# Moving the attention of the even chunks between the FFN groups of a fused mLSTM and squared-ReLU FFN kernel

## The chip, the cores and the metric

The kernel runs on one core of a Trainium2 chip. A core has five engines, each with its own in-order instruction queue: PE (TensorE, matrix multiplication), DVE (VectorE), ACT (ScalarE), POOL (GpSimd) and SP (SyncE, which here only issues transfers). POOL issues transfers too, from the same queue that holds its arithmetic. The metric is the device time of one execution in microseconds (us).

## The reference

```python
# per step t, for each of 4 x 8 (batch, head) pairs, D = 40, S = 768
m_new  = max(f + m, i)
C = exp(f + m - m_new) * C + exp(i - m_new) * v k^T
n = exp(f + m - m_new) * n + exp(i - m_new) * k
y = sigmoid(o) * (C q) / max(|n q|, 1)
# then x = y as (3072, 320), and
h = max(x @ w_in, 0)          # (3072, 2048)
out = (h * h) @ w_out         # (3072, 320)
```

All is float32; the two weights arrive as 64-bit floats and are rounded in the kernel.

## The kernel before, in words

Tokens are cut into 24 chunks of 128 (six for each batch). A chunk's recurrence is computed as masked attention inside the chunk plus a state C that is carried from one chunk to the next. Two chunks make a group of 256 tokens, of which there are 12; the FFN works by group. FFN1 (x times w_in) and FFN2 (h² times w_out) use a Strassen-like scheme, whose sums of inputs and weights other engines prepare.

The main loop (from line 1430 on) is an order of work written out by hand. It walks a list `parts` of quarter steps: four steps of FFN2 for one group, then four of FFN1 for the group two further on, and so on. Each four steps are a window, and each window also carries one chunk `s` of attention: **even chunks go with an FFN2 window, odd chunks with an FFN1 window** (`fast` in the code). `at` is the quarter step, 0 to 3. [...]

For one chunk the attention has these parts:

- `pair_up` (line 338; the DMAs L343) copies keys and queries into DRAM in another order. From chunk 10 on POOL issues it, four DMAs for a chunk. `load_squares` (L398, SP, four DMAs) reads them back as 32x32 squares, and `turn_kq` (L405, DVE) transposes them. There are two such buffers, for even and odd chunks.
- `load` (L363, L365, L375) brings keys and values: seven DMAs, issued by POOL.
- `load_A` (L429, two DMAs on SP) brings the decay logarithms A. `decays` (L496, four instructions on ACT) takes their exponentials, `mask` (L478, two on POOL) masks A, `weigh` (L509, eight on ACT) turns A into weights and calls `values` (L530, POOL), `decay_C` (L767, POOL) decays the state.
- `scores` (L586, 32 PE instructions) multiplies keys and queries, `weighted` (L608, two on DVE) multiplies scores and weights, `scale_q` (L762, DVE) scales the queries.
- `attend_begin` (L800, L820, L831) and `attend_end` (the same lines) are the two halves of the product with values and state. Between them stands L791, a tiny DVE instruction that reads the first half's result and so keeps the second half behind it. After `attend_end` DVE turns and copies the result (L854, L861).
- `store_num` (L869), `load_num` (L874), both SP, take the result through DRAM; `normalise_turned` (L886 to L899, DVE) divides; `store_rows` (L927) and `load_rows` (L932) take it through DRAM again; `turn_squares` (L939, DVE) transposes it to be the FFN's input. `sums_of_x` (L1125, L1128; five POOL instructions) then makes the sums `xs` of a group that FFN1 of the next window needs.

All attention matmuls have 64 rows or fewer, and so have the last 64 of the 320 input rows of FFN1 (`ffn1_rows`, L1166). The rest of the FFN (L1133 for FFN1, L1057 for FFN2) uses 128 x 128 matmuls. FFN1 does two halves of a group in one window: `ffn1_open` (four products X, Y, V, Z of eight instructions; Y and V read sums made by POOL, Y reads `xs[3]`), then `ffn1_close` (three products, and `ffn1_rows` for the second half). FFN2 does seven products of 16 instructions in four steps; in step 0 ACT copies the first product out of its bank (L1077) before step 1 adds to that bank.

Around the change the order per window, PE's part first, is:

- even window: `scores(s)` at the top, FFN2 step 0, `attend_begin(s)`, `scores(s+1)`, `attend_end(s)`, FFN2 steps 1 to 3.
- odd window: open, `attend_begin(s)`, `ffn1_rows`, `attend_end(s)`, close; open, close with `ffn1_rows`.
- POOL in an even window: `mask(s+1)`, `decay_C(s+1)`, `load(s+3)` at step 1; `values(s+1)` at step 2; `sums_of_x`, `pair_up(s+3)`, `pair_up(s+4)`, `load(s+4)` at step 3; then in the odd window `mask(s+1)` for the next even chunk, and so on.
- SP in an even window: `store_num`, `load_num`, `load_squares(s+2)`, `load_A(s+2)`; output; `store_rows`, `load_rows`; output. In an odd window: `store_num`, `load_num`, `load_squares(s+2)`; `store_rows`, `load_A(s+2)`, `load_rows`.

Of the kernel before, what the change touches and what calls it, by code (L numbers as in the profile page):

```python
# [29 lines left out]
def kernel(  # L30
# [30 lines left out]
    NB = S // P  # L61
    NT = B * NB
# [340 lines left out]
    def turn_kq(s):  # L403
        t = kqT_b[s % NKT][:].rearrange("p n j t -> p (n j t)")
        nc.vector.transpose(t, t)  # L405
# [192 lines left out]
    def weighted(s):  # L598
        d = st[s]
        d["P"] = []  # L600
        for i in range(2):
            heads = slice(i, H, 2)
            t = d["W"][:, heads, :] if s < ROT else d["W"][:, i::2, DP:]
            if s < W_IN:
                at = 2 * H * P + W * (2 * (s % 2) + i)
                t = flat_c[:, at : at + W].rearrange("p (j t) -> p j t", j=PR)
            d["P"].append(t)
            nc.vector.tensor_tensor(t, d["sc"][i], d["W"][:, heads, :] if s < ROT else t, op=ALU.mult)  # L608
# [522 lines left out]
    def blocks(to, lhsT, rhs, q, start):  # L1131
        for n in range(4):
            nc.tensor.matmul(  # L1133
                to[:, n, :], lhsT=lhsT[:, 4 * q + n, :], rhs=rhs, start=(start and n == 0), stop=True,
                skip_group_check=True,
            )
# [17 lines left out]
    def ffn1_rows(g, q, first):  # L1154
        xT, xs = st["xT", g], st["xs"]
        X, Y, V, Z = st["f1"]
        lo, hi = HALVES
        pairs = (
            ((X, lo, xT[lo, 0, 2, :], False), (Y, hi, xT[hi, 1, 2, :], first)),
            ((V, lo, xT[lo, 1, 2, :], first), (Z, hi, xs[hi, 1, :], False)),  # L1160
        )
        for pair in pairs:
            for n in range(4):
                for cols in HALVES:
                    for to, rows, rhs, start in pair:
                        nc.tensor.matmul(  # L1166
                            to[cols, n, :], lhsT=w_in2[rows, 4 * q + n, cols], rhs=rhs,
                            start=(start and n == 0), stop=True, skip_group_check=True,
                        )

    def ffn1_close(g, q, begun):
        xT, xs = st["xT", g], st["xs"]
        (X, Y, V, Z), (U2, U4) = st["f1"], st["U"]
        g4 = st["g2", g][:, 8 * q : 8 * q + 8, :].rearrange("p (n two) t -> p n two t", two=2)
        t0, t1 = slice(0, P), slice(P, 2 * P)
        blocks(X, F12, xT[:, 0, 1, :], q, False)
        blocks(Y, F21, xs[:, 2, :], q, not begun)
        blocks(V, WS[3], xT[:, 1, 1, :], q, not begun)
        if not begun:
            ffn1_rows(g, q, False)  # L1180
        tt = nc.vector.tensor_tensor
        nc.scalar.activation(g4[:, :, 0, t0], X[:], AF.Relu)  # L1182
        tt(U2[:], U2[:], Y[:], op=ALU.add)
        tt(g4[:, :, 1, t1], U4[:], Y[:], op=ALU.add)
        tt(g4[:, :, 0, t1], U4[:], V[:], op=ALU.add)
        tt(g4[:, :, 1, t0], U2[:], Z[:], op=ALU.subtract)
        st["open"] = g4
# [16 lines left out]
    def do(f, s):  # L1204
        if 0 <= s < NT:
            f(s)
# [97 lines left out]
    for u in range(8):  # L1304
        s = 2 + u // 2
# [114 lines left out]
    for g in range(NG):  # L1420
        parts += [(2, g, i) for i in range(4)]
        if g + 2 < NG:
            parts += [(1, g + 2, i) for i in range(4)]
    ROUNDED = (17, 18)
    assert ROUNDED[-1] == len(pieces)

    for n, (which, g, i) in enumerate(parts):
        s, at = NB + n // 4, n % 4
        if n == len(ROUNDED):
            brought.close()  # L1430
            late = ctx.enter_context(tc.tile_pool(name="late", bufs=1, side="right"))
        even = s % 2 == 0
        fast = which == 1
        if n == 2:
            half_tanh(6)
            half_tanh(7)
        if at == 0 and even:
            do(scores, s)
            if n > 0:
                do(turn_kq, s + 1)  # L1440
            do(weighted, s)
        if n == 0:
            turn_kq(7)
            pair_up(8)
            load_rows(4)
            rounding.words()
            rounding.join()
        if at == 1:
            do(attend_begin, s)
            if n == 5:  # L1450
                sums_of_weights(3)
            if even:
                do(lambda s: scores(s, ("h", "h")), s + 1)
            if fast:
                ffn1_rows(g, 0, True)
            do(attend_end, s)
            do(decays, s + 1)
            do(mask, s + 1)
            if not even and not fast:
                do(turn_kq, s + 1)  # L1460
            do(decay_C, s + 1)
            if not fast and not even:
                do(turn_squares, s - 1)
            if even and s > NB:
                do(load, s + 3)
            do(store_num, s)
            if n == 1:
                normalise_turned(5)
                store_rows(5)
                turn_squares(4)  # L1470
            if n == 5:
                load_rows(6)
            do(load_num, s)
            if n == 1:
                load_rows(5)
                weigh(7, masked=True)
                sums_of_win(2)
            do(load_squares, s + 2)
            if even:
                do(load_A, s + 2)  # L1480
        if n == 3:
            load_o(8)
            load_o(9)
            sums_of_weights(0)
        if n == 8:
            sums(1, slice(0, NPAIR), (3,))
        if n == 9:
            sums(1, slice(0, NPAIR), (4,))
            sums_of_weights(2)
            turn_squares(6)  # L1490
        if which == 2 and i == 3 and g == NG - 2:
            sums(g + 1, slice(0, NPAIR), (2,))
        if which == 2 and g > 1 and i < 2:
            sums(g, slice(0, NPAIR), (3 + i,))
        if at == 3 and even and NB < s and s // 2 - 1 < NG:
            sums_of_x(s // 2 - 1)
        if at == 2 and not fast:
            if even and n > 2:
                do(turn_squares, s - 1)
            do(scale_q, s + 1)  # L1500
        if at == 3:
            if s % 4 == 3:
                for r in range(s + 1, min(s + 5, NT) if n > 7 else 10):
                    half_tanh(r)
        if n == 10:
            half_tanh(10)
            half_tanh(11)
        if fast:
            if i % 2:
                if n == 7:  # L1510
                    sums(1, slice(0, NPAIR), (2,))
                ffn1_close(g, i // 2, i == 1)
                if at == 1:
                    do(turn_kq, s + 1)
                    if n > 5:
                        do(turn_squares, s - 1)
            else:
                ffn1_open(g, i // 2)
                if i == 0 and g > 2:
                    sums(g - 1, slice(0, NPAIR), (2,))  # L1520
            if at == 2:
                do(scale_q, s + 1)
            if n == 6:
                sums(1, slice(0, NPAIR), (1,))
        elif g == 0:
            ffn2(i)
        else:
            ffn2_fast(g, i)
        if at == 2:
            if n > 2:  # L1530
                do(lambda s: weigh(s, masked=True), s + 1)
            ffn1_square()
            if even:
                do(weighted, s + 1)
            do(normalise_turned, s)
            do(store_rows, s)
            if n == 2:
                pair_up(9)
                turn_squares(5)
                sums_of_x(2)  # L1540
                load(8)
            if not even:
                do(load_A, s + 2)
            if n > 2:
                do(load_o, s + 5)
                do(load_rows, s)
            if s == NB + 1:
                pair_up(s + 3)
        if n in (5, 6):
            load(4 + n)  # L1550
            load_o(5 + n)
        if even and at == 3 and s > NB:
            do(pair_up, s + 3)
            do(pair_up, s + 4)
        if even and at == 3 and s > NB:
            do(load, s + 4)
        if n == 4:
            sums_of_weights(1)
        if n == 3:
            turn_halves()  # L1560
        if n in (12, 25):
            spread_slots(2 + n // 25)
        if at == 0:
            ffn1_square()
        if n < len(ROUNDED):
            while rounding.done < ROUNDED[n]:
                rounding.step()
# [30 lines left out]
```

## Time and profile before

| what | value |
|---|---|
| time, median of 3 runs | 485.88 us (484.6 to 485.91) |
| profiled execution's own time | 488.72 us |
| its span (first to last instruction) | 487.0 us |
| TensorE clock granted | 1.00 |
| PE busy | 475.4 us, 98% of the span |
| DVE busy | 339.5 us, 70% |
| ACT busy | 243.3 us, 50% |
| POOL busy | 227.1 us, 47% |
| DMA moved | 69.93 MB, mean 144 GB/s |

A time in the profile is counted from the first instruction. "PE" rows are matmuls, "SPq" rows are transfers being issued by SP, and an issue on POOL stands among POOL's own rows. In the timeline a row merges neighbouring instructions of one line; its columns are start, length (both us), engine, line, operation, destination <- sources, shape and count. The chain is followed back from the last instruction, at each step to what released it.

The windows that the change touches begin at 125.3 us (FFN2 with chunk 8) and end at 421.2 us (FFN2 with no chunk left). A pair of windows, even and odd, takes 36.2 to 37.0 us in the profile, except one pair in which PE stood still for 1.88 us at 224.8 us with no releaser shown.

### The profile page before, as it was taken

To read this page: it belongs to the slowest core of one execution; us is meant where nothing else is said; L and a number is where in the kernel's file an instruction comes from. 1 tells how busy PE (TensorE), PEld (TensorE's weight loads), DVE (VectorE), ACT (ScalarE), POOL (GpSimd) and SP (SyncE) were. 2 spreads that over 40 slices of the span, in tenths; PEclk is the share of its full clock that TensorE was granted. 3 is DMA by queue.
4 is the path that set the end of the run, shared out by engine and by line. 5 is a ranking of instruction groups with operands and counts; after the bars stand their busy time and mean duration, and the time that the engine had idled before them with its cause. 6 is when DMAs were issued, how large, how long until landed. Compare 5 with 4: busy or idle time off the path is not lost.

```text
span 487.0 us, 15731 instructions
## 1 busy us (share of the span) xinstructions
PE 475.4 (98%) x6389; PEld 442.6 (91%) x6389; DVE 339.5 (70%) x725; ACT 243.3 (50%) x534; POOL 227.1 (47%) x337
## 2 busy tenths in 40 slices
PE   8989999999999999998999999999999999999997
PEld 4876787779899999998999999999999999999997
DVE  7869768798897766765966956766956956635441
ACT  4698898535733722922732941742942640513300
POOL 5454554656598096098088088089074040020000
PEclk9999999999999999999999999999999999999999
DMA  8999998779988867777759668668646612200000
GB/s 179 235 243 248 265 202 213 198 145 214 185 158 181 138 124 201 136 137 186 133 105 221 132 107 203 140 116 205 137 98 160 126 46 82 57 24 6 1 28 27
DMA packets 192696, 69.93 MB, mean 144 GB/s; under 512 B 158128, under 2 KB 181360, under 8 KB 192624
## 3 DMA queue, kind: packets, MB, share of 16 engines
q1 hardware_dynamic: 186400, 58.68, 55.9%
q0 software_dynamic: 6080, 10.16, 9.1%
q8 instruction: 50, 0.82, 0.7%
q14 instruction: 22, 0.18, 0.2%
q10 hardware_dynamic: 144, 0.10, 0.1%
HBM read 55.69 MB, written 18.92 MB: 153 GB/s over the span
## 4 chain that ended last, share of the span: by engine, by line
PE 74%; DMA 7%; DVE 5%; ACT 4%; SPq 4%; issue 3%; POOL 2%; DVEq 0%; POOLq 0%; ACTq 0%
PE h_ps L1057 32%; PE h_ps L1133 20%; PE h_ps L1166 6%; PE h_ps L973 3%; PE numT L820 2%; PE numT L800 2%; DMA kqT<-kq_rows 2%; DMA raw<-in_moe_w_out_dram 1%; PE numT L831 1%; DMA lent_t<-in_moe_w_in_dram 1%; SPq L398 1%; DMA kq_rows<-in_k_dram 1%; ACT g_c L515 1%; SPq L413 1%; PE tp L554 1%
## 5 line engine op out<-in xcount | busy, mean ns | idle before, releaser
L478 POOL TENSOR_SCALAR_AFFINE_SELECT A_bc<-A_bc 64x512 f32<-64x512 f32 x32 | 23.0, 720 | 89.3 <-ACT kq L496 70.9
L1147 ACT COPY r_sb<-h_ps 128x512 f32<-128x512 f32 x20 | 11.7, 586 | 84.7 <-PE h_ps L1133 84.7
L1057 PE MATMUL h_ps<-T,S 128*128 128x160 f32 x352 | 51.7, 300 | 0.1
L1057 PEld LDWEIGHTS h_ps<-T,S 128*128 128x128 f32 x352 | 48.9, 190 | 0.6 <-ACT g L1182 0.5
L1057 PE MATMUL h_ps<-w_out,g 128*128 128x160 f32 x336 | 49.2, 303 | 0.0
L1057 PEld LDWEIGHTS h_ps<-w_out,g 128*128 128x128 f32 x336 | 46.1, 190 | 1.3 <-issue 0.7
L1073 DVE TENSOR_TENSOR y_sb<-y_sb,h_ps 128x160 f32<-128x160 f32 x44 | 14.1, 320 | 45.5 <-PE h_ps L1057 45.2
L1133 PE MATMUL h_ps<-xT,w_in 128*128 128x128 f32 x320 | 43.3, 278 | 1.6 <-issue 1.6
L1133 PE MATMUL h_ps<-lent_t,w_in 128*128 128x128 f32 x320 | 42.3, 275 | 0.0
L1133 PEld LDWEIGHTS h_ps<-xT,w_in 128*128 128x128 f32 x320 | 39.2, 192 | 3.2 <-issue 2.9
L375 POOL DMA_DIRECT2D va<-in_v_dram x64 | 39.1, 619 | 1.9 <-DMA kq_rows<-in_k_dram 1.3
L1166 PE MATMUL h_ps<-xT,w_in 64*64 64x128 f32 x960 | 39.2, 272 | 0.0
L1133 PE MATMUL h_ps<-lent_t 128*128 128x128 f32 x320 | 39.1, 275 | 0.0
L1133 PEld LDWEIGHTS h_ps<-lent_t,w_in 128*128 128x128 f32 x320 | 38.9, 192 | 0.0
L1133 PEld LDWEIGHTS h_ps<-lent_t 128*128 128x128 f32 x320 | 37.3, 192 | 0.2 <-issue 0.2
L1166 PEld LDWEIGHTS h_ps<-xT,w_in 64*64 64x64 f32 x960 | 34.8, 133 | 1.3
L509 ACT ACTIVATE A_bc<-A_bc,b_R 128x64 f32<-128x64 f32 (+1 forms) x128 | 35.7, 361 | 0.5 <-POOL A_bc L478 0.2
L854 DVE STREAM_TRANSPOSE tn<-numT 128x256 f32<-128x256 f32 x36 | 14.0, 428 | 27.3 <-PE numT L800 18.5
L1125 POOL TENSOR_TENSOR lent_t<-xT 128x128 f32<-128x128 f32 (+1 forms) x18 | 15.6, 887 | 32.7 <-DVE xT L939 32.7
L973 PE MATMUL h_ps<-xT,w_in 128*128 128x256 f32 x128 | 29.9, 386 | 0.4 <-POOL w_in L236 0.4
L1057 PE MATMUL h_ps<-w_out,g_c 128*128 128x160 f32 x192 | 28.0, 302 | 0.0
L973 PEld LDWEIGHTS h_ps<-xT,w_in 128*128 128x128 f32 x128 | 23.5, 190 | 4.5 <-POOL w_in L236 0.8
(231 smaller groups left out, 1145.9 us busy)
## 6 DMA issues: line engine op xcount, KB each, us to landing
A_bc<-a_slots SPq DMA_DIRECT2D x32, 256.0 KB, 4.5
kq<-num_rows SPq DMA_DIRECT2D x80, 64.0 KB, 2.3
num_rows<-tn SPq DMA_DIRECT2D x18, 256.0 KB, 2.5
raw<-in_moe_w_out_dram SPq DMA_DIRECT2D x7, 640.0 KB, 5.1
kqT<-kq_rows SPq DMA_DIRECT2D x34, 128.0 KB, 3.7
og<-in_o_gate_dram SPq DMA_DIRECT2D x24, 160.0 KB, 5.3
x_rows<-x_sb SPq DMA_DIRECT2D x20, 192.0 KB, 3.3
xT<-x_rows SPq DMA_DIRECT2D x80, 48.0 KB, 3.4
```

Of the source, the lines that this page charges most:

```text
L375: eng.dma_start(dst[HALVES[n], PR * (1 - late_keys) : PR * (2 - late_keys)], src[HALVES[late_keys], PR * m : PR * (m + 1)],)
L478: nc.gpsimd.affine_select(part, part, compare_op=ALU.is_ge, fill=-1e30, base=0, pattern=[[0, PR], [0, 2], [1, DP]], channel_multiplier=-1,)
L509: nc.scalar.activation(A[0][:, x, to], A[0][:, x, to], AF.Exp, bias=b_R[:, b, c, own, x : x + 1],)
L800: nc.tensor.matmul(d["numT"][m][HALVES[e], i, :], lhsT=C[LIVE[i], at : at + DP], rhs=d["eA"][LIVE[i], j, :], start=(i == m), stop=False, s ...
L854: nc.vector.transpose(to[:, 2 * m : 2 * m + 2], d["numT"][m].rearrange("p c t -> p (c t)"))
L973: nc.tensor.matmul(hs[i][:, n, :], lhsT=w_in[:, a, fb * P : (fb + 1) * P], rhs=xT[:, :, a, :], start=(n == 0 and a == 0), stop=False,)
L1057: nc.tensor.matmul(to, lhsT=lhsT[:, p], rhs=rhs[:, p, :], start=(start and p == 0), stop=(p == NPAIR - 1), skip_group_check=True,)
L1073: add = lambda to, a, b: nc.vector.tensor_tensor(to, a, b, op=ALU.add)
L1125: sub = lambda to, a, b: eng.tensor_tensor(to, a, b, op=ALU.subtract)
L1133: nc.tensor.matmul(to[:, n, :], lhsT=lhsT[:, 4 * q + n, :], rhs=rhs, start=(start and n == 0), stop=True, skip_group_check=True,)
L1147: nc.scalar.copy(m1[:], X[:])
L1166: nc.tensor.matmul(to[cols, n, :], lhsT=w_in2[rows, 4 * q + n, cols], rhs=rhs, start=(start and n == 0), stop=True, skip_group_check=True,)
```

## The change

From chunk 10 on (`EARLY = 10`) an even chunk is called `joined`, which holds for 10, 12, ... 22. For a joined chunk `s`:

- `scores(s)` moves from the top of its even window into the odd window before, between `ffn1_rows` and `attend_end(s-1)`; its two banks come one from each pool.
- `weigh(s)` and `weighted(s)` are emitted before the second `ffn1_open` of that odd window, `turn_kq(s+1)` behind it.
- `attend_begin(s)` is emitted inside the second `ffn1_close`, between its three products and its `ffn1_rows`.
- `scores(s+1)`, `attend_end(s)` and what follows them on the other engines (`decays(s+1)`, `mask(s+1)`, `decay_C(s+1)`, `load(s+3)`, `store_num`, `load_num`, `load_A(s+2)`) move from step 1 of the even window to step 0, ahead of FFN2's first product. FFN2's seven products then follow one another on PE.

Besides, `load_squares` for chunks from 11 on is emitted in the odd windows, at step 0 for the odd chunk and at step 3 for the even one; `turn_kq` of a joined chunk at step 3 of the even window before; and the two `pair_up` of every even window from chunk 8 on at step 1 instead of step 3.

```diff
-    def ffn1_close(g, q, begun):
+    def ffn1_close(g, q, begun, between=None):
...
         blocks(V, WS[3], xT[:, 1, 1, :], q, not begun)
+        if between:
+            between()
         if not begun:
             ffn1_rows(g, q, False)
...
+    EARLY = 10
+    def joined(s):
+        return EARLY <= s < NT and s % 2 == 0
...
-        if at == 0 and even:
+        if at == 0 and not even and s + 2 > EARLY or at == 3 and not even and s + 3 > EARLY:
+            do(load_squares, s + (2 if at == 0 else 3))
+        if at == 0 and even and s < EARLY:
             do(scores, s)
...
-        if at == 1:
-            do(attend_begin, s)
+        if at == (0 if joined(s) else 1):
+            if not joined(s):
+                do(attend_begin, s)
...
             if even:
-                do(lambda s: scores(s, ("h", "h")), s + 1)
+                do(lambda s: scores(s, ("h" if s < EARLY else False, "h")), s + 1)
             if fast:
                 ffn1_rows(g, 0, True)
+                if joined(s + 1):
+                    scores(s + 1, (False, "h"))
             do(attend_end, s)
...
-            do(load_squares, s + 2)
+            if s + 2 <= EARLY:
+                do(load_squares, s + 2)
...
         if at == 3:
+            if joined(s + 2):
+                turn_kq(s + 2)
...
-                ffn1_close(g, i // 2, i == 1)
+                early = (lambda: attend_begin(s + 1)) if at == 3 and joined(s + 1) else None
+                ffn1_close(g, i // 2, i == 1, early)
                 if at == 1:
-                    do(turn_kq, s + 1)
+                    if s + 1 < EARLY:
+                        do(turn_kq, s + 1)
...
             else:
+                if at == 2 and joined(s + 1):
+                    weigh(s + 1, masked=True)
+                    weighted(s + 1)
                 ffn1_open(g, i // 2)
+                if at == 2 and joined(s + 1):
+                    do(turn_kq, s + 2)
...
-            if n > 2:
+            if n > 2 and not joined(s + 1):
                 do(lambda s: weigh(s, masked=True), s + 1)
...
-        if even and at == 3 and s > NB:
+        if even and at == 1 and s > NB:
             do(pair_up, s + 3)
             do(pair_up, s + 4)
```

## The prediction

> **What bounds the kernel now.** I read the page's busy shares, the chain that ended last, then the timelines of PE and POOL over the windows of chunks 14 and 15 and of SP and DVE behind them.
>
> ```profile
> PE 475.4 (98%) x6389; PEld 442.6 (91%) x6389; DVE 339.5 (70%) x725; ACT 243.3 (50%) x534; POOL 227.1 (47%) x337
> ```
>
> ```profile
> 176.59 1.23 POOL va L375 x2
> 177.83 2.10 POOL lent_t L1125 x2
> 180.83 4.39 DMA kq_rows<-in_k_dram
> ```
>
> PE is full, so a saving on PE counts, as long as nothing else comes to set the pace. The chain shows who is nearest to that: it leaves PE in chunk 10's window and runs through POOL, a load (L375), `sums_of_x` (L1125), then `pair_up`. The same stretch one pair later:
>
> ```profile
> 245.20 1.46 POOL L478 TENSOR_SCALAR_AFFINE_SELECT A_bc<-A_bc 64x512 f32<-64x512 f32 x2 [10.99 <-ACT kq L496]
> 246.74 1.31 POOL L767 TENSOR_TENSOR Cd<-C,kq 128x164 f32<-128x164 f32 x1
> 248.00 0.79 POOL L363 DMA_DIRECT2D kq<-in_k_dram  x1
> 248.79 1.23 POOL L365 DMA_DIRECT2D kq<-in_k_dram  x2
> 250.01 2.44 POOL L375 DMA_DIRECT2D va<-in_v_dram  x4
> 252.46 0.76 POOL L530 TENSOR_TENSOR vw<-va,A_bc 128x328 f32<-128x328 f32 x1
> 253.16 2.15 POOL L1125 TENSOR_TENSOR lent_t<-xT 128x128 f32<-128x128 f32 x2
> 255.27 0.45 POOL L1128 TENSOR_TENSOR lent_t<-lent_t,xT 128x128 f32<-128x128 f32 x1
> 255.80 0.48 POOL L1125 TENSOR_TENSOR lent_t<-lent_t,xT 128x128 f32<-128x128 f32 x1
> 256.23 1.06 POOL L343 DMA_DIRECT2D kq_rows<-in_k_dram  x2
> ```
>
> ```profile
> 240.66 2.34 PE L1057 MATMUL h_ps<-T,S 128*128 128x160 f32 x16
> 242.92 0.45 PE L800 MATMUL numT<-kq,C 40*64 40x128 f32 x8
> ...
> 245.33 4.61 PE L1057 MATMUL h_ps<-w_out,g 128*128 128x160 f32 x32
> 249.78 2.34 PE L1057 MATMUL h_ps<-T,S 128*128 128x160 f32 x16
> ...
> 256.30 1.05 PE L1133 MATMUL h_ps<-xT,w_in 128*128 128x128 f32 x8
> 257.19 1.95 PE L1133 MATMUL h_ps<-lent_t 128*128 128x128 f32 x16
> ```
>
> POOL runs without a gap from the mask on. Its L1128 makes xs[3], done at 255.72; PE wants it for product Y at 257.19. The slack is 1.47 us. The same subtraction (start of Y less end of L1128) gives 2.57 us for the window of chunk 8, 2.17 for 10, 0.61 for 12, 2.17 for 16, 1.55 for 18, 1.57 for 20. For 22, where POOL has nothing to load, it is 4.4. The eight `pair_up` issues stand **behind** the sums now, from 256.23 to 260.32.
>
> ```profile
> 274.32 0.38 SPq L927 DMA_DIRECT2D x_rows<-x_sb  x1
> 274.81 1.10 SPq L429 DMA_DIRECT2D A_bc<-a_slots  x2
> ```
>
> This sets when the odd chunk's A comes, and so when POOL's stretch can begin: `load_A(17)` waits on SP behind `store_rows(15)`; its two halves land at 279.0 and 280.2.
>
> **What PE gains.** Now a pair of windows has three runs of 64-row matmuls, after the change two. Going into and out of one: FFN2's 16-instruction product takes 2.17 us undisturbed (249.78 to the next start) and 2.26 before the run (240.66 to 242.92); the 32 after it take 4.45 against 4.35; the run's own last rows 0.33 against 0.22 to 0.26. With the scores' exit (0.78 against 0.69) that is 0.32 us. Seven joined chunks: 7 x 0.32 = 2.2 us, the whole gain if PE stays the pace-maker. The Trainium skill, "TensorEngine Tiling (Array Packing)", Key Properties, says that changing the tiling mode drains TensorE, and gives no price; the rows above are the price here.
>
> **What moves on POOL.** The two `pair_up` of an even window go ahead of `values` and `sums_of_x`. Eight issues at 0.51 us (256.23 to 260.32) make 4.1 us by which the sums come later, unless POOL's stretch begins sooner; the slack is 0.6 to 2.6 us. For chunk 20 only `pair_up(23)` is left, 2.05 us; for 22 none. The Trainium skill, "DMA: Bandwidth & Descriptors", Issuing engines are not separate DMA queues, calls the time of issuing usually small beside the transfer itself: by it the order on POOL would hardly matter and 2.2 us of gain would stand. The POOL rows say otherwise: they follow one another serially, arithmetic and issues.
>
> **Does POOL's stretch begin sooner?** Its block is emitted one FFN2 step earlier (about 4.6 us), but the mask needs `decays`, and these need A. I count from the first FFN1 matmul of the odd window (256.30 for chunk 15). After the change `attend_end(15)` ends 0.69 later, since `scores(16)` (32 instructions, 0.69) stands ahead of it, at 7.8. DVE then holds: four sums of the first close, beginning 0.69 later than now (265.54 less 256.30 is 9.24), 9.9 to 12.3 (2.4 for four, rows 265.54 to 267.93); `turn_squares` 0.5; `weighted(16)` 0.95; two sums of the second open 1.25; `turn_kq(17)` 1.2; `scale_q(16)` 0.7; so `normalise_turned(15)` begins at 16.9 at the earliest and takes 1.95 (272.35 to 274.30): 18.85. Now it ends at 18.0. `store_rows(15)` then, A's second half 5.9 later as here (274.32 to 280.21): 24.8 to 25.2. Decays of that half 0.72, mask of it 0.73: POOL is done with the mask at 26.3 to 26.7. Now that is at 27.1 (283.43 less 256.30; 26.7 to 27.1 in the other windows). POOL leads by 0.3 us; I take this, between -1.2 (SP late, below) and 1.5 (normalising as early as now, so that A lands at 23.9 and nothing of ACT's squares stands ahead of the decays).
>
> **The sum by windows,** each 4.1 less its slack less the lead: chunk 8 (attention not moved, no lead) 1.5; 10: 1.6; 12: 3.2; 14: 2.3; 16: 1.6; 18: 2.25; 20: 2.05 - 1.57 - 0.3 = 0.2. In these the PE saving counts nothing, for POOL sets the end. Chunk 22: PE sets it, minus 0.32 plus the wait of the next paragraph, 0.4. Together 13.0 us.
>
> **Other moved waits.** ACT's copy of FFN2's first product (L1077) is now queued behind `decays(s+1)`, and step 1 cannot add to that bank before it. Decays end at about 25.9, the copy at 26.2; PE, which starts FFN2 at 21.1, wants step 1 at 25.6: some 0.7 us, inside POOL's wait except in the window of 22. So FFN2 is not quite unbroken.
>
> `weigh(16)` (eight, 2.23) ahead of the second open's copy on ACT: it ends at 11.9, the copy at 12.5, and the next product on that bank is at 14.2; hidden. `attend_begin(16)` wants `scale_q(16)` at 16.95 where it ends at 16.9: 0 to 0.3, hidden by the later wait. L791 stands behind `normalise_turned(15)`: ready at 19.1, PE asks at 20.3. `load_squares(17)` (2.3 to 4.1 us of issuing) goes ahead of `store_num(15)` on SP: it may delay that by up to 3 us, but DVE could not normalise before 16.9 anyway. `load_squares(18)`, now ahead of `store_num(16)`, costs at most 2 us there, and `normalise_turned(16)` waits for PE's step 2 as now. The even chunk's `load_A` comes sooner, its squares too: no one waits. The banks that scores take are read by `weighted` long before; 0.
>
> **Against the runs.** The profiled execution took 488.72 (487.0 span, 1.7 around it); with 13.0 it would be 501.7. The median is 2.84 lower, of which 1.88 may be the unexplained PE stop. I add the 13.0 to the median: **498.9 us**.
>
> **Rivals.**
> - POOL leads far more, the sums come in time and PE's 2.2 us stay: 483.7. For it: the block is emitted 4.6 us earlier. Against: A lands when it does. It decides at a lead of about 2.8 us (4.1 less the common slack of 1.6, plus 0.3 for the faster PE), which needs A's second half by 22.8, before the 23.9 of now. 8%.
> - The `pair_up` issues hide, as a transfer of no weight, and only ACT's late copy costs: seven times (0.7 - 0.32), 488.5. Against: the serial rows. 6%.
> - Lead 1.5 instead of 0.3 in the windows of 10 to 18 (5 x 1.2 = 6.0 less), and PE's gain of 0.32 in the last two in place of 0.2 and 0.4 (1.2 less): 5.8 over the median, 491.7. 11%.
> - SP becomes the pace-maker: squares ahead of `store_num`, and a landing of 4.5 us as at 264.4, push normalising 1.5 us past DVE's own order: lead -1.2, in six windows (10 to 20) 9.0 more: 507.9. 17%.
> - The forecast, lead about 0.3 give or take 0.8: 495 to 503. 58%.
>
> **How the numbers follow.** The range leaves out the first rival and reaches a little past the fourth: 488 to 510. What can be told from no change is about 0.3%, 1.5 us. Faster: the first rival, 8%. Same: the edge between first and second, 3%. Slower: 89%.
>
> **What would show it.** Right: in PE's waits a wait of product Y (L1133, reading lent_t) on POOL L1128, 1 to 3 us in the windows of chunks 8 to 18 and none at 22; `pair_up` rows ahead of L1125 on POOL; PE of the window of 8 already late by 1.5. A short stop of PE before L1057's step 1 on ACT L1077. Two runs of 64-row matmuls for a pair. Wrong: POOL's mask begins 4 us sooner relative to the odd window, or L1128 ends before PE asks.

## The result, and the profile after

| | before | after |
|---|---|---|
| median | 485.89 us (484.6 to 488.61, 4 runs) | 503.12 us (502.51 to 509.59, 4 runs) |
| ratio | | 1.0365, 95% interval 1.0309 to 1.0421 |
| profiled execution | 488.72 us, span 487.0 | 503.39 us, span 501.7 |
| granted TensorE clock, mean | 1.00 | 0.997 |

The change makes the kernel 3.65% slower. The page of after, its busy shares and, from part 4, the shares of the chain by engine:

```profile
PE 478.2 (95%) x6387; PEld 445.1 (89%) x6389; DVE 339.0 (68%) x725; ACT 243.2 (48%) x534; POOL 220.7 (44%) x337
...
PE 47%; DMA 19%; SPq 10%; POOL 8%; DVE 7%; ACT 4%; issue 3%; DVEq 0%; POOLq 0%; ACTq 0%
```

PE does the same work in a longer span, and the chain that ended last is on PE for less than half of it. The rest is transfers, SP's issuing, POOL and DVE: in many of the windows the small steps of the attention have become the pace-maker. The waits of PE's weight loads (engine, tile, line, what released it; us in total, how often, longest) say where PE stands for them:

```profile
PEld h_ps L1057 <- ACT y_sb L1077: 6.8, 5, 2.2
PEld h_ps L1133 <- POOL lent_t L1128: 5.4, 4, 2.5
...
PEld numT L831 <- DVE kq L791: 2.5, 4, 1.2
...
PEld h_ps L1166 <- DVE r_sb L1149: 1.4, 1, 1.4
```

Two places stand out: FFN2's step 1 behind ACT's copy of the first product (L1077), and product Y behind POOL's sum (L1128). The first lies in the even window and the second right behind its end, so what PE has lost at the first it doesn't lose again at the second. The chain through one odd and the next even window (start, us, what) shows that both hang on one string, here from chunk 17 to the sums that FFN1 needs:

```profile
316.38 2.92 DMA num_rows<-tn
...
320.61 1.91 DMA kq<-num_rows
...
325.66 5.22 DMA A_bc<-a_slots
330.90 0.73 ACT kq L496 x2
...
332.49 1.31 POOL Cd L767
...
338.19 2.55 POOL kq_rows L343 x6
...
341.22 1.02 POOL kq_rows L343 x2
342.25 0.76 POOL vw L530
343.01 1.09 POOL lent_t L1125 x2
344.10 0.41 POOL lent_t L1128
...
344.56 1.49 PE h_ps L1133 x11
```

Read backwards: Y starts 0.05 us after L1128 ends; ahead of the sums on POOL stand the eight `pair_up` issues (338.19 to 342.24, 4.05 us); POOL's stretch begins with the mask, behind `decays`, behind A's load; A's issue stands on SP behind `store_rows`, which waits for the normalising, and that for the round trip of the numerator (316.38 to 322.52). For the sums of the windows of chunks 8, 10, 12, 16 and 18 Y starts within 0.06 us of L1128's end; in that of 14 L1128 ends 0.27 us before Y starts, and Y does not wait. Why the string starts so late is to be seen on SP and DVE in the same odd window (start, us, engine, line, operation, tiles, count; in brackets the idle time before and what ended it):

```profile
312.49 3.80 SPq L398 DMA_DIRECT2D kqT<-kq_rows  x4
316.38 0.51 SPq L869 DMA_DIRECT2D num_rows<-tn  x1
319.31 1.73 SPq L874 DMA_DIRECT2D kq<-num_rows  x4
324.60 0.38 SPq L927 DMA_DIRECT2D x_rows<-x_sb  x1
325.15 1.09 SPq L429 DMA_DIRECT2D A_bc<-a_slots  x2
```

```profile
312.05 0.78 DVE L854 STREAM_TRANSPOSE tn<-numT 128x256 f32<-128x256 f32 x2 [1.10 <-PE numT L820]
322.64 0.17 DVE L886 TENSOR_SCALAR dm<-kq 128x8 f32<-128x8 f32 x1 [2.20 <-DMA kq<-num_rows]
```

DVE has turned the numerator by 312.83. SP is then issuing the squares of chunk 19, until 316.29, and issues `store_num` only behind them, 12.2 us after the window's first FFN1 matmul (304.17); DVE stands idle for 2.20 us before it can normalise, at 18.5. The same window before, whose first FFN1 matmul is at 293.26:

```profile
302.86 0.39 SPq L869 DMA_DIRECT2D num_rows<-tn  x1
306.21 1.74 SPq L874 DMA_DIRECT2D kq<-num_rows  x4
```

```profile
309.60 0.17 DVE L886 TENSOR_SCALAR dm<-kq 128x8 f32<-128x8 f32 x1 [2.10 <-DMA kq<-num_rows]
```

There `store_num` goes out at 9.6 and normalising begins at 16.3. DVE waits for the numerator there too, so its idle time alone is no sign of the change; that `store_num` goes out 2.6 us later and normalising begins 2.1 us later is.

### The profile page after: what moved, and what is told of

The parts are those of the page before. It is cut to its first block, busy times and chain, and to the rows that moved or that the text cites. A ratio compares the mean times of both kernels' runs of the same rounds, so it can differ in the third digit from the quotient of the medians.

```text
span 501.7 us, 15692 instructions
## 1 busy us (share of the span) xinstructions
PE 478.2 (95%) x6387; PEld 445.1 (89%) x6389; DVE 339.0 (68%) x725; ACT 243.2 (48%) x534; POOL 220.7 (44%) x337
## 4 chain that ended last, share of the span: by engine, by line
PE 47%; DMA 19%; SPq 10%; POOL 8%; DVE 7%; ACT 4%; issue 3%; DVEq 0%; POOLq 0%; ACTq 0%
PE h_ps L1057 17%; PE h_ps L1133 13%; DMA A_bc<-a_slots 6%; DMA num_rows<-tn 5%; DMA kq<-num_rows 4%; PE h_ps L1166 4%; PE h_ps L973 4%; SPq L874 3%; SPq L932 2%; POOL kq_rows L343 2%; SPq L398 2%; POOL va L375 2%; PE numT L820 2%; SPq L429 1%; PE numT L800 1%
## 5 line engine op out<-in xcount | busy, mean ns | idle before, releaser
L1133 PE MATMUL h_ps<-lent_t 128*128 128x128 f32 x320 | 40.8, 282 | 4.6 <-POOL lent_t L1128 4.6
L1133 PEld LDWEIGHTS h_ps<-lent_t 128*128 128x128 f32 x320 | 38.4, 197 | 5.6 <-POOL lent_t L1128 5.4
L496 ACT ACTIVATE kq<-A_bc 64x256 f32<-64x256 f32 x56 | 20.1, 406 | 44.5 <-DMA A_bc<-a_slots 44.3
L1133 PEld LDWEIGHTS h_ps<-xT,w_in 128*128 128x128 f32 x320 | 39.2, 192 | 1.6 <-issue 1.2
L1184 ACT ACTIVATE g<-h_ps 128x512 f32<-128x512 f32 x12 | 7.1, 594 | 49.9 <-PE h_ps L1133 38.6
L1057 PEld LDWEIGHTS h_ps<-w_out,g_c 128*128 128x128 f32 x192 | 26.4, 190 | 3.2 <-ACT y_sb L1077 2.6
```

Source lines behind the costliest of these rows:

```text
L496: nc.scalar.activation(e[rows, j : j + 2, :], A[rows, i::2, own * P : (own + 1) * P], AF.Exp)
L1057: nc.tensor.matmul(to, lhsT=lhsT[:, p], rhs=rhs[:, p, :], start=(start and p == 0), stop=(p == NPAIR - 1), skip_group_check=True,)
L1133: nc.tensor.matmul(to[:, n, :], lhsT=lhsT[:, 4 * q + n, :], rhs=rhs, start=(start and n == 0), stop=True, skip_group_check=True,)
```

## The experiments

Two theories. **POOL**: the `pair_up` issues ahead of the sums set the pace, as forecast. **SP**: the squares ahead of `store_num` make normalising, `store_rows` and A late, and with them all that hangs on A. Every kernel below is the changed one with the edit shown, where nothing else is said; ratios are to before (medians of 485.05 to 486.16 us, taken beside each run), with their 95% intervals.

**1. The pairs back.**

```diff
-        if even and at == 1 and s > NB:
+        if even and at == 3 and s > NB:
             do(pair_up, s + 3)
```

> The changed kernel with one part undone: the two pair_up of an even window again at step 3, behind sums_of_x. POOL theory (the eight issues ahead of the sums set the pace): product Y no longer waits for L1128 and the time falls by about 11 us, to 489 to 492. SP theory (load_squares ahead of store_num makes normalising, store_rows and the odd chunk's A late, and the decays that wait for A now hold up the copy L1077): the 5.4 us of waits on L1128 go, but PE then arrives sooner at the wait on L1077, which grows by much of that; 498 to 501.

495.64 us, 1.0223 (1.0172 to 1.0274): 7.5 of the 17.2 us are gone. No wait on L1128 is left; the largest is

```profile
PEld h_ps L1057 <- ACT y_sb L1077: 9.1, 6, 2.1
```

So the pairs cost what they were said to at the sums, but without them 9.5 us remain over before, and PE's waits at the copy grow. Neither theory alone holds the whole.

**2. The pairs alone,** in the kernel before: `at == 3` to `at == 1` for the two `pair_up` and nothing else.

> The kernel before with this one part of the change: pair_up at step 1 of the even window. POOL theory: 4.1 us less the slack of each window (1.5, 1.9, 3.5, 1.9, 2.6 and 0.5 for chunks 8, 10, 12, 16 and 14/18, 20, no lead), 14 us together: 498 to 501. SP theory: no more than the waits on L1128 that the changed kernel shows, 5 us: 488 to 492.

505.21 us, 1.0378 (1.0318 to 1.0438), above the 498 to 501 expected. This one line costs as much as the whole change. Waits of PE's weight loads:

```profile
PEld h_ps L1133 <- POOL lent_t L1128: 14.8, 6, 4.9
```

The rows of POOL, and the matmul that waits, in the window of chunk 12:

```profile
220.37 1.05 POOL L343 DMA_DIRECT2D kq_rows<-in_k_dram  x2
221.39 1.03 POOL L343 DMA_DIRECT2D kq_rows<-in_q_dram  x2
222.40 1.03 POOL L343 DMA_DIRECT2D kq_rows<-in_k_dram  x2
223.40 1.03 POOL L343 DMA_DIRECT2D kq_rows<-in_q_dram  x2
...
227.69 1.14 POOL L1125 TENSOR_TENSOR lent_t<-xT 128x128 f32<-128x128 f32 x2
228.78 0.45 POOL L1128 TENSOR_TENSOR lent_t<-lent_t,xT 128x128 f32<-128x128 f32 x1
```

```profile
229.29 1.01 PE L1133 MATMUL h_ps<-lent_t 128*128 128x128 f32 x3 [4.68 <-POOL lent_t L1128]
```

The 14.8 us of waits are what the serial issues explain (14 was expected). On top of them comes TensorE's clock: with three of these stops it was granted at 0.5 for 3.4, 6.8 and 3.4 us. From Y's start to the first attention matmul PE took 4.32, 5.09 and 4.50 us in these windows, against 2.88 behind the waits without a slow stretch: some 5 us lost (an estimate from these rows). That waits and clock together exceed the 18 fits before's own stop of 1.88 us, which this profile does not have.

Runs 1 and 2 together say that the costs do not add: the pairs cost 18 by themselves and 7.5 on top of the rest of the change. They lie on one string, and what is late by one is not late again by the other.

**3. The squares in the gap.** In the odd window the squares are issued while the numerator's store is under way:

```diff
-        if at == 0 and not even and s + 2 > EARLY or at == 3 and not even and s + 3 > EARLY:
-            do(load_squares, s + (2 if at == 0 else 3))
+        if at == 3 and not even and s + 3 > EARLY:
+            do(load_squares, s + 3)
...
             do(store_num, s)
+            if not even and s + 2 > EARLY:
+                do(load_squares, s + 2)
```

> The changed kernel with the odd chunk's load_squares between store_num and load_num, where SP waits for the store to land anyway, instead of ahead of store_num. POOL theory: the mask comes hardly sooner, 501 to 503. SP theory: store_num goes out some 3 us sooner, the waits on L1077 (6.8 us) and on L791 (2.5 us) go: 493 to 497.

496.53 us, 1.0224 (1.0173 to 1.0275): 6.6 us gained. The copy's waits fall from 6.8 to 2.7 us, those for the sums stay:

```profile
PEld h_ps L1133 <- POOL lent_t L1128: 6.0, 3, 3.4
PEld h_ps L1057 <- ACT y_sb L1077: 2.7, 5, 0.9
```

In the odd windows of chunks 9 to 21 `store_num` went from 10.96 to 13.94 us after the window's start to 8.96 to 12.37, and DVE normalises without waiting for the numerator in all of them but that of 11 (0.62 us). In the window of chunk 17, whose first FFN1 matmul is at 298.33 here:

```profile
307.29 0.34 SPq L869 DMA_DIRECT2D num_rows<-tn  x1
```

```profile
315.06 0.13 DVE L886 TENSOR_SCALAR dm<-kq 128x8 f32<-128x8 f32 x1
```

So SP's order is a cause too, and part of the copy's waits is its mark.

**4. A in the gap:** `load_A(s+2)` of odd chunks from 11 on emitted right behind `store_num(s)` instead of behind `store_rows(s)`.

> The changed kernel with the odd chunk's load_A between store_num and load_num instead of behind store_rows. Both theories have the late A in the middle: it lands some 8 us sooner, the decays no longer hold up L1077, and POOL's mask can start 4 us sooner, which makes up for the pair_up. POOL theory: 485 to 488 with a wait left at chunk 8 alone. SP theory: the waits on L1077 go, those on L791 stay (normalising is still late): 489 to 494.

500.42 us, 1.0311 (1.0262 to 1.0359), a miss for both. Of the copy's waits 0.5 us is left, but the squares still stand ahead of `store_num`, and now A's two issues ahead of `load_num`: the normalising comes no sooner in most windows (in that of chunk 17 at 18.7 us after its start, against 18.5), and L791 behind it on DVE holds up `attend_end`:

```profile
PEld numT L831 <- DVE kq L791: 7.0, 4, 3.2
PEld h_ps L1133 <- POOL lent_t L1128: 4.2, 3, 3.4
```

Three of these waits (3.43, 3.17 and 2.19 us) came with 3.4 us each at a granted clock of 0.5.

**5. The decays behind the copy:** in joined windows `decays(s+1)`, `mask(s+1)`, `decay_C(s+1)` and `load(s+3)` emitted after FFN2's step 0, so that ACT copies first.

> The changed kernel with decays, mask, decay_C and load of the even window emitted behind FFN2's step 0, so that ACT copies FFN2's first product before it waits for A; POOL's order within itself stays. If the copy's wait only shows the lateness of A, PE then arrives sooner at the sums and waits there (L1128) instead: 500 to 503. If the copy's wait is a cost of its own: its 6.8 us go, 495 to 497.

501.88 us, 1.0311 (1.0247 to 1.0375). No wait on L1077 is left, and the time hardly moves:

```profile
PEld h_ps L1133 <- POOL lent_t L1128: 11.8, 6, 3.6
PEld numT L831 <- DVE kq L791: 2.8, 3, 1.3
```

What PE no longer waits for at the copy it waits for at the sums (5.4 to 11.8 us); this profile has 10.2 us at a granted clock of 0.5, that of the changed kernel 3.4. The copy is a symptom; the string A, decays, mask, POOL's row, sums sets the pace.

**6. Both back:** edits 1 and 3 together.

> The changed kernel with two parts undone: pair_up behind the sums again, and the odd chunk's load_squares between store_num and load_num. If the squares ahead of store_num are what makes A late, A lands some 2 to 3 us sooner than with the pairs alone put back (495.6), the waits on L1077 (9 us there) shrink to 1 to 2: 486 to 490. If A is late for the place of load_A behind store_rows alone, little changes: 493 to 496.

491.44 us, 1.0128 (1.0076 to 1.0181), between the two forecasts: 11.7 of the 17.2 us, less than 7.5 and 6.6 added up. The largest wait for another engine is

```profile
PEld h_ps L1057 <- ACT y_sb L1077: 2.7, 5, 1.2
```

**7. Pairs back and A behind `load_num`,** the squares still ahead of `store_num`.

> The changed kernel with pair_up behind the sums again and the odd chunk's load_A right behind load_num, so that it no longer waits on SP for normalising and store_rows; the squares stay ahead of store_num. If late A is the cause of what the pairs alone leave (495.6), all waits on L1077 go and PE keeps its saving but for the waits on L791 behind late normalising (2 to 3 us): 485 to 489. If normalising late is as bad by itself: 492 to 495.

496.96 us, 1.0218 (1.0163 to 1.0273), no better than the pairs alone put back, and above both forecasts. An early A does not mend a late normalising, which shows at L791 (this profiled execution took 502.83 us, 5.9 above the median, so its waits are not those of the median):

```profile
PEld numT L831 <- DVE kq L791: 5.8, 6, 2.9
PEld h_ps L1166 <- DVE r_sb L1149: 3.4, 1, 3.4
```

**8. All three:** edits 1 and 3, and A behind `load_num`.

> The changed kernel with pair_up behind the sums again, the odd load_squares between store_num and load_num, and the odd load_A right behind load_num. With no engine late PE sets the pace, with one run of 64-row matmuls fewer in each of seven pairs: 0.32 us x 7 less than before and its own waits gone, 482.5 to 485, a little faster than the kernel before. If something else holds it: 486 to 490.

491.5 us, 1.0114 (1.0077 to 1.0152), a miss for both forecasts. With pairs and squares in place, A's order is worth nothing that can be told. But the late engines are gone from most windows: pairs of windows, from one odd window's start to the next, take 39.69, 35.51, 38.34, 36.57, 36.59, 36.45 and 37.54 us. Before they take 36.77, 36.21, 38.46 (with the stop of 1.88), 36.96, 36.52, 36.96 and 36.77; the second and the fifth are shorter, since chunks 12 and 18 begin a batch and have no state to multiply. The first is long because `weigh(10)` is late: its ACT instructions wait 2.94 us for POOL's mask, ahead of which POOL still issues `a_slots` (155.24 to 157.01), and PE then waits for ACT and DVE (1.16, 1.04 and 0.66 us). The third holds two stops, of 0.95 and 0.87 us from one matmul's start to the next, the fifth one of 1.15 and the last one of 0.81, that nothing on the other engines explains:

```profile
PEld h_ps L1057 <- issue: 2.2, 7, 1.1
PEld numT L831 <- issue: 1.7, 3, 0.8
```

**9. From chunk 12 on:** the same with `EARLY = 12`, so that the first, long pair is left as before.

> The three repairs together (pair_up behind the sums, squares in the gap, load_A behind load_num), with the new order beginning at chunk 12 instead of 10, and load_A moved from chunk 11 on. With the three repairs alone (491.5) the pair of chunks 9 and 10 took 39.69 us against 36.77, 2.9 more, since POOL still had spread_slots ahead of mask(10). Theory that this start is the rest: 488 to 489. Theory that the long runs of 64-row matmuls cost in the middle too, because PE runs out of instructions (four stops of 0.8 to 1.1 us with no releaser, each half a microsecond behind an instruction fetch): these stops stay, so no better than 488, and slower than the kernel before (485) although PE's switches are fewer. Without that cost it would be 483 to 485.

488.89 us, 1.0048 (1.0023 to 1.0073), which both theories allow. The stops without a releaser are still there, as the second has it: four of 0.45 to 1.15 us; they are read from a profiled execution of 494.57 us, 5.7 above the median.

**10 to 12. Shifting the program.** The stops named "issue" come in or right behind long runs of small matmuls, and PE goes on 1.2 to 1.6 us after the end of a DMA of 16,384 bytes on queue 8, an instruction queue. The page of after:

```profile
q8 instruction: 50, 0.82, 0.7%
```

If PE ran out of instructions there, more instructions at the program's start must move the stops to other windows. Before the first weights arrive PE runs idle matmuls; the edit gives `idle` a width and cuts the same idle columns into smaller pieces, 36 matmuls more (72 instructions) or 84 more (168):

```diff
-    idle(12)
+    idle(48, W // 4)
```

Experiment 9 with 72 more instructions:

> As the kernel that starts at chunk 12, but the first 12 idle matmuls of 512 columns on PE are 48 of 128 columns: the same PE time at the start, 72 more PE instructions, so that the 256-instruction blocks of PE's program fall elsewhere against the runs of 64-row matmuls. Fetch theory: stops with no releaser move to other windows, each again 0.5 us behind a fetch; total 487 to 491. If the stops come from something else in those windows (a bank, a queue), they stay in the same windows.

486.69 us, 1.0009 (0.9983 to 1.0035). With 168 more:

> As the kernel that starts at chunk 12, with 96 idle matmuls of 64 columns at the start: 168 more PE instructions. Fetch theory: again other windows for the stops, 486 to 492; otherwise the same windows.

488.56 us, 1.0036 (1.0001 to 1.007). The kernel before with 72 more:

> The kernel before with the same 72 more instructions at the start, as a control. Both: within 1.5 us of 485, since its runs of 64-row matmuls are 96 to 144 matmuls long and seldom outrun a fetch (one such stop, 1.88 us, in the profile before).

484.73 us, 0.9973 (0.9951 to 0.9994).

The stops moved each time: from the windows of chunks 13, 14, 18 and 21 (experiment 9) to those of 15 and 16 with 72 instructions, to that of 19 with 168; in before, the one at 224.79 was gone. In all three shifted kernels there is a new one, of 0.55 to 0.82 us, at about 113 us, ahead of the windows that the change touches. With more PE instructions queue 8 shows 51 packets in place of 50, so it is PE's. PE's timeline with 72, in the run of 64-row matmuls of chunk 15's window:

```profile
261.69 0.35 PE L831 MATMUL numT<-vw,kq 64*64 64x41 f32 x12
261.85 0.43 PE L820 MATMUL numT<-A_bc,va 64*64 64x64 f32 x12
263.82 0.27 PE L820 MATMUL numT<-A_bc,va 64*64 64x64 f32 x2 [1.54 <-issue]
```

It stops between two matmuls of one line, with no other engine named, and goes on 1.49 us after a fetch ended. Over all these stops PE halts anywhere from 0.4 us before a fetch's end to 0.9 behind it, but goes on 1.22 to 1.63 us behind it. That is what waiting for the fetched piece would look like; no view shows PE's store of instructions itself.

A pair of windows without such a stop takes 36.45 to 36.6 us in experiments 8 and 10, against 36.77 to 36.96 before (pairs with chunk 12 or 18 left out).

No version of the change beats the kernel before: experiment 10, the change with most of its delays taken out, equals it, and before with the same shift (experiment 12) is 0.27% below before, at the edge of what these runs resolve, and 2.0 us, 0.4%, below experiment 10. Shift against shift the repaired change is still slower.

## Why the prediction was right, and where it wasn't

The direction and the size held, and so did the main mechanism, the `pair_up` issues ahead of the sums: 503.1 us lie 4.2 above the forecast of 498.9, just past the upper edge of its own 495 to 503 and inside the range. But a second mechanism, which the forecast costed at nothing and the fourth rival named, was at work too, and another error made up for part of it. Step by step:

**The sum.** The lateness of product Y grew from window to window by the amounts below (difference of Y's starts in the two profiles).

| window of chunk | 8 | 10 | 12 | 14 | 16 | 18 | 20 | 22 | sum |
|---|---|---|---|---|---|---|---|---|---|
| predicted, us | 1.5 | 1.6 | 3.2 | 2.3 | 1.6 | 2.25 | 0.2 | 0.4 | 13.0 |
| measured, us | 1.45 | 1.72 | 3.53 | 0.83 | 3.41 | 2.95 | 0.45 | 0.33 | 14.67 |

Five windows are within 0.35 us. Those of 16 and 18 were 1.8 and 0.7 us worse than predicted; the masks ahead of them come 2.7 and 1.6 us late (below). That of 14 can't be judged: the kernel before has its PE stop of 1.88 us there, and the changed kernel a stretch of slow clock (about 1.6 us lost) and two shorter stops (0.70 and 0.36 us).

**The pairs on POOL: right,** in place and price. Y waits on L1128 from the first window, the eight issues take 4.05 us where 4.1 was reckoned, and the line alone slows the kernel by 3.78%. The sign that was named, a wait of Y of 1 to 3 us in the windows of 8 to 18, came in that form only in those of 8 and 12 (1.96 and 2.49 us) and as 0.73 us in that of 18; elsewhere PE had lost the time at the copy already. The Trainium skill, "DMA: Bandwidth & Descriptors", Issuing engines are not separate DMA queues, calls issuing usually small beside the transfer. For one transfer the trace agrees (0.51 us beside a median of 4.0 from issue to landing for `kq_rows`), but that the order on POOL would then hardly matter does not follow: with arithmetic behind them in the same queue, eight issues in a window made 14.8 us of PE's waits over six windows (run 2).

**"DVE could not normalise before 16.9 anyway": the wrong conclusion.** This is the step by which the squares ahead of `store_num` were costed at nothing. The bound itself is about right: in run 3, with the squares out of the way, DVE begins to normalise in chunk 17's window at 16.7 (315.06 less 298.33) without a wait. The delay of `store_num` is about right too: 12.2 in place of 9.0 in run 3, where "up to 3 us" was said. What was left out is the numerator's way through DRAM. From `store_num`'s issue to the normalising 6.3 us pass (316.38 to 322.64), so with `store_num` at 12.2 DVE gets its input at 18.5, not at 16.9. Run 3 shows the price, 6.6 us in all. So POOL did not lead by 0.3. The mask of the odd windows of chunks 9 to 19 ended, counted from the window's start, 2.6, 0.2, 2.2, 2.7, 1.6 and 0.4 us later than before. PE's own stops blur these: with before's stop of 1.88 us and the changed kernel's waits for the sums in those of 9, 13 and 19 (2.04, 2.57 and 0.82) taken off, 1.0 us later on average, and less if the slow clock in that of 13 and a wait of 1.39 us in that of 15 are taken off too. That is on the side of the fourth rival's -1.2, not of the forecast's 0.3.

**What made up for it.** From the mask's end to L1128's end POOL took 9.06 us before (246.66 to 255.72); with 4.1 more it would be 13.2; it took 12.1 (332.40 to 344.51). The first two sums lasted 1.15 us instead of 2.15, which had been carried over unchanged. In the windows of 10, 14, 16, 18 and 20 before, the first sum alone took 1.42 to 1.54 us: it ran beside DVE's L1052 and ended about 0.3 us behind it. In their new place, up to the window of 20, the sums meet no L1052, and the first takes 0.46. Whether L1052 is what held POOL up was not tried; in the window of 8 before, the first sum ran beside it too and took 0.46. Two terms were mis-sized by about a microsecond in several windows with opposite signs, so the good sum is in part luck.

**The copy: right in kind, too small.** A stop of 0.7 us a window inside POOL's wait was expected; it was 6.8 us in five windows, 0.8 to 2.2 each, because the decays were late with A. That it lies inside the same lateness was right, as run 5 shows.

**L791: wrong.** "Ready at 19.1, PE asks at 20.3" became four waits of 2.5 us in all: again the late normalising, for L791 stands behind it.

**PE's gain: about right in size, and lost.** 0.32 us a pair was reckoned; experiments 8 and 10 show 0.2 to 0.5 in the pairs that can be compared. It was rightly left out of the sum, since PE did not set the end. Even with most delays out, as in experiment 10, it went to two stops of PE for instructions, 1.76 and 0.51 us, which the prediction did not know, and to a wait of 1.1 us for DVE (L1149) in the first joined window.

**From the profiled run to the median.** The profiles differ by 14.67 us, the medians by 17.23: before's profiled execution was 2.83 above its median and after's only 0.27 above. That is 2.6 of the 4.2 us of the miss; the other 1.7 are 14.67 less 13.0.

In all, of the 17.2 us, 11.7 are the pairs and the squares together (experiment 6) and some 2.6 the first pair of windows (8 to 9). What the step from 9 to 10 gained, 2.2 us, was not settled: the stops for instructions in the windows of the change add up to 2.9 us in the profile of 9, to 2.3 in that of 10 and to 1.25 in that of 11, while the medians are 488.89, 486.69 and 488.56. That the stops move with the program is shown; that their sum makes these three times differ is not.

## What to carry to other kernels

An issue of a transfer is an instruction like any other on its queue: before moving one, list what stands behind it on that engine and how much slack that has, and do so for every queue the move touches, SP too. "It is hidden, since the next engine is busy until then" holds only if that engine's own row has no wait in it; look for who is late next and not for who is late now. When a string of small steps already runs with less than 2 us to spare, removing the wait that shows (here the copy's, in experiment 5) moves it along the string, and only what starts the string sooner or takes work out of it shortens the time.

## What the runs showed of the hardware

**PE seems to run out of instructions.** Queue 8 brings PE's instructions in pieces of 16,384 bytes. In or right behind long runs of 64-row matmuls (a weight load and a matmul each, 19 to 27 ns a pair on average; runs of 96 to 144 before, 144 to 176 in the joined windows) PE stopped for 0.36 to 1.88 us and went on 1.2 to 1.6 us after such a fetch had ended; adding instructions at the start moved the stops. Longer runs of small matmuls are thus not free. The Trainium skill, "Runtime: NRT & Kernel Launch", Instruction fetch mechanics, tells of blocks of 16 KiB, which agrees with these fetches, and calls the cost of crossing one "mostly hidden"; the stops above are where it was not.

**The clock can fall with a stop of 2 us.** In the profiles of after and of experiments 1 to 11, from 45 us on, 11 of 18 stops of PE of 2.0 us or more (from one matmul's start to the next) came with 3.4 or 6.8 us at a granted clock of 0.5; of 41 stops between 1 and 2 us one did (1.94 us). In the first 45 us it fell at about 33 us in four of these profiles, where no stop was longer than 1.8 us. In after it was the stop of the window of chunk 12; the columns are the stretch, its length, busy us (and instructions) of PE, PEld, DVE, ACT and POOL, PE's clock, DMA's share and GB/s:

```profile
core 0: us, PE busy (x) PEld busy (x) DVE busy (x) ACT busy (x) POOL busy (x), PEclk, DMA share, GB/s
222.08:226.00 3.92, 1.62 (x15) 1.43 (x14) 2.01 (x7) 2.02 (x5) 3.77 (x8) 1.00 0.60 214
226.00:229.40 3.40, 3.40 (x19) 3.40 (x18) 3.23 (x10) 0.00 (x0) 3.40 (x6) 0.51 0.45 99
229.40:232.80 3.40, 3.40 (x117) 3.28 (x120) 1.87 (x3) 0.00 (x0) 2.90 (x4) 0.99 1.04 156
```

PE stood 2.57 us in the first stretch and then did 19 matmuls in 3.4 us at half the clock. The Trainium skill, "TensorE: Matmul & The Clock Gate", What's actually happening, puts the fall after at least one idle window of about 3.4 us. The length of the slow stretches agrees with that window; stops of 1.94 to 2.57 us sufficed for the fall here, while two of 3.45 and 3.5 us had none. Such a stretch under FFN1's first matmuls cost 1.6 us (4.50 us in place of 2.88 from Y's start to the first attention matmul, in after and in run 2), which makes a wait of 2 us on PE dearer than it looks.
